# Changing the PSUM banks of three G_B tiles and of B's denominators in a gated mix of two linear-attention blocks

## The chip, the cores and the metric

The kernel runs on one core of one Trainium2 chip. The metric is the time of one execution on the device, in microseconds (us), given as the median of several runs. The core has a matrix engine (TensorE, PE in the profile; PEld is its row for weight loads), a vector engine (VectorE, DVE), a scalar engine (ScalarE, ACT), GpSimd (POOL) and a queue engine (SyncE, SP) that issues transfers. Matmuls write into PSUM, which this kernel holds as eight banks of 128 partitions x 512 fp32; ACT and DVE read results out of it ("evict" them) into SBUF.

## The reference

Both blocks see the same input x (2048 x 640, bf16), each with its own weights; 32 heads of 20 columns.

```python
def block(x, wqkv, wo):                      # A and B alike
    q, k, v = heads(x @ wqkv)                # H = 32, Dh = 20
    phi = lambda t: jnp.where(t > 0, t + 1, jnp.exp(t)) + 1e-6
    pq, pk = phi(q), phi(k)
    kv  = einsum("bhsd,bhse->bhde", pk, v)
    z   = einsum("bhsd->bhd", pk)
    num = einsum("bhqd,bhde->bhqe", pq, kv)
    den = einsum("bhqd,bhd->bhq", pq, z)[..., None] + 1e-6
    return merge(num / den) @ wo

g = sigmoid((x * gate_w).sum(-1, keepdims=True))
out = g * block(x, A_wqkv, A_wo) + (1 - g) * block(x, B_wqkv, B_wo)
```

## The kernel before, in words

The kernel never forms v. For each block X it computes PK = phi(k) in 16 row tiles (`k_tile`), PQ = phi(q) transposed in 20 tiles of 128 x 512 (`q_tile`), and G = x^T PK, a 640 x 640 matrix in five row tiles j (`g_piece`). From G it gets M = WV^T G, masked to the heads (`m_part`), then WP = M^T WO in five tiles (`wp_tile`), so that the result is one more matmul of PQ with WP (`fin_mm`). The denominators (`den`, line 637) are PQ times ZBD, the sums of PK spread out by head; DVE copies them out with eps added (line 652), takes four reciprocals (line 660), SP stores these and loads them back widened to all columns (`widen`, line 672), and DVE multiplies PQ by them (`scale`, lines 699 and 707). At the end `fin_a` (ACT, line 793) scales A's final tile by the gate, `fin_out` (DVE, line 805) adds B's, and SP stores the rows.

The eight PSUM banks are four pairs: `PP[0]` is banks 0 and 1 (the first pair), `PP[1]` banks 2 and 3, `PP[2]` banks 4 and 5, `PP[3]` banks 6 and 7 (the fourth pair). A G tile fills a pair: 512 columns in one bank and 128 in the other. It is built from four pieces q of eight matmuls (four row tiles, a 128x512 and a 128x128 matmul for each); after the fourth piece ACT evicts the whole tile to GT (line 577). A `wp_tile` also fills a pair, half a tile in each bank: ACT evicts the half in the first bank of the pair and DVE the one in the second (both line 759). Tiles 0 to 4 of WP A use the pairs 1, 2, 3, 1, 2 (line 891), those of WP B the pairs 0, 3, 1, 0, 3 (line 936). A's final tiles alternate between `PP[2]` and `PP[1]`, B's between `PP[0]` and `PP[3]` (line 768). Both halves of M_B use banks 7 and 6 (lines 932 and 933).

The order of work is that of the Python calls. A small scheduler (`_Sched`, line 72) records each call's reads and writes by key, PSUM keys being banks, and each engine runs its own operations in that order, waiting by semaphore for the last writer and all readers of what it touches; PE does not wait for PE (line 110). `_interleave` (line 192) deals out a list `mains` one entry at a time and slips in the stages of side chains at given positions. In `mains` the 20 q tiles of B come three at a time with one piece of G_B after each three, until five pieces are placed (line 884): the four of tile 0 and the first of tile 1. From `nB` on (line 885) the other 15 pieces of G_B follow (line 887). The chain at `nB + 1` (line 920) puts `wp_a_den_b` (line 889) behind the third piece of G_B's tile 1. So PE's order around the change is

- pieces 1 and 2 of G_B's tile 1; the five tiles of WP A; the denominators of B; piece 3 of tile 1, and its eviction
- the pieces of G_B's tiles 2, 3 and 4, while DVE scales A's queries
- A's final tiles 0 and 1, M_B, A's final tile 2, the five tiles of WP B, and then the final tiles of A and B in turn to the end

(pieces and tiles counted from 0 in the code; in words the tiles are the first to the fifth.) G_A, earlier in the kernel, uses the pairs 1, 0, 1, 0, 1 for its five tiles. All matmuls but the transposes are recorded by one helper, so the profile shows them under line 302, told apart by their operands: `ps<-PKB,XN` is G_B, `ps<-PQB,ZBD` the denominators of B, `ps<-WKA,MG` and `ps<-WKB,MG` WP A (its WO rows are kept in the old WK buffers), `ps<-GT,WVB` M_B, `ps<-WPA,PQA` the final tiles of A.

Of the kernel before, what the change touches and what calls it, by code (L numbers as in the profile page):

```python
# [205 lines left out]
def bass_gated_mix__linear_attn_block__linear_attn_block__prompt_kernel(  # L206
# [18 lines left out]
    with ExitStack() as es:  # L225
# [44 lines left out]
        def bank(i, lo, hi, p0=0, p1=128):  # L270
            o = 512 * (i % 2)
            return PP[i // 2][p0:p1, o + lo : o + hi]
# [23 lines left out]
        def mms(steps, reads=(), writes=(), name=""):  # L296


            def fn(pe):
                ins = None  # L300
                for o, l, r, st, sp, tp in steps:
                    ins = pe.matmul(o, l, r, start=st, stop=sp, tile_position=tp)  # L302
                return ins

            return sch.op("PE", fn, reads=reads, writes=writes, name=name)
# [5 lines left out]
        def act(fn, reads=(), writes=(), name=""):  # L311
            return sch.op("ACT", fn, reads=reads, writes=writes, name=name)

        def dve(fn, reads=(), writes=(), name=""):
            return sch.op("DVE", fn, reads=reads, writes=writes, name=name)
# [245 lines left out]
        def g_piece(X, j, q, pp):  # L561
            P = PP[pp]
            bks = [("PS", 2 * pp), ("PS", 2 * pp + 1)]
            steps = []
            for t in range(4 * q, 4 * q + 4):
                l = XN[:, t, 128 * j : 128 * j + 128]
                steps.append((P[:, 0:512], l, PK[X][:, t, 0:512], t == 0, t == NT - 1, None))
                steps.append((P[:, 512:D], l, PK[X][:, t, 512:D], t == 0, t == NT - 1, None))
            mms(
                steps,  # L570
                reads=[("XN", t) for t in range(4 * q, 4 * q + 4)] + [("PK", X, t) for t in range(4 * q, 4 * q + 4)],
                writes=bks,
                name="g%s%d%d" % (X, j, q),
            )
            if q == 3:
                act(
                    lambda e: e.activation(GT[:, j, :], P[:, 0:D], ACT.Copy),  # L577
                    reads=bks,
                    writes=[("GT", j)],
                )  # L580
# [56 lines left out]
        def den(X, bk):  # L637
            xi = BR.index(X)
            steps = []
            for k in range(NC):  # L640
                for b in range(NB):
                    o = bank(bk, 0, 512, 32 * b, 32 * b + 32)
                    r = PQ[X][:, k, 512 * b : 512 * b + 512]
                    steps.append((o, ZBD[:, NC * xi + k, :], r, k == 0, k == NC - 1, (0, 32 * b)))
            mms(
                steps,
                reads=[("ZBD", X)] + [("PQ", X, b, k) for k in range(NC) for b in range(NB)],
                writes=[("PS", bk)],
                name="den%s" % X,
            )  # L650
            dve(
                lambda e: e.tensor_scalar(DT32[:, :], bank(bk, 0, 512), EPS, None, op0=ALU.add),
                reads=[("PS", bk)],
                writes=[("DT",)],
            )

        def recip(i):
            def rcp(e):
                with nc.allow_low_precision(reason="r goes into a bf16 matmul"):
                    return e.reciprocal(RC[:, 128 * i : 128 * i + 128], DT32[:, 128 * i : 128 * i + 128])  # L660

            dve(rcp, reads=[("DT",)], writes=[("RC", i)])
# [76 lines left out]
        def wp_tile(X, k, pp):  # L739
            P = PP[pp]  # L740
            cells = []
            for g in range(4):
                w = 8 + g // 2 if k == 4 else 4 * (k // 2) + g
                fs = slice(32 * (g % 2), 32 * (g % 2) + 32) if k == 4 else slice(k % 2, 64, 2)
                cells.append((w, MG[:, w, fs]))
            for j, (lo, hi) in enumerate(((0, D // 2), (D // 2, D))):
                mms(
                    [
                        (P[32 * g : 32 * g + 32, 512 * j : 512 * j + hi - lo], l, wo_at(X, w)[0][:, lo:hi], True, True, (0, 32 * g))
                        for g, (w, l) in enumerate(cells)  # L750
                    ],
                    reads=[("WO", X, w) for w, _ in cells] + [("MG", w) for w, _ in cells],
                    writes=[("PS", 2 * pp + j)],
                    name="wp%s%d" % (X, k),
                )
            for j, (lo, hi) in enumerate(((0, D // 2), (D // 2, D))):
                o, p = WP[X][:, k, lo:hi], P[:, 512 * j : 512 * j + hi - lo]
                (dve if j else act)(
                    lambda e, o=o, p=p, j=j: e.tensor_copy(o, p) if j else e.activation(o, p, ACT.Copy),  # L759
                    reads=[("PS", 2 * pp + j)],  # L760
                    writes=[("WP", X, k, j)],
                )
# [105 lines left out]
        mains = []  # L868
# [9 lines left out]
        while qs:  # L878
# [3 lines left out]
            if len(qs) > 2:  # L882
                j, q = gs.pop(0)
                mains.append(lambda j=j, q=q: g_piece("B", j, q, 0))
        nB = len(mains)
        for j, q in gs:
            mains.append(lambda j=j, q=q: g_piece("B", j, q, 1 if j == 3 else 0))

        def wp_a_den_b():
            for k in range(NC):  # L890
                wp_tile("A", k, (1, 2, 3)[k % 3])
            den("B", 7)
            for i in range(4):
                recip(i)

        def den_a():
# [23 lines left out]
                nB + 1,  # L920
                [
                    (0, wp_a_den_b),
                    (0, lambda: widen("B")),
                ],
# [65 lines left out]
```

## Time and profile before

| what | us |
|---|---|
| median of 3 runs (lowest, highest) | 195.71 (195.59, 196.29) |
| the profiled execution, whole | 196.04 |
| its span, first to last instruction | 194.3 |
| PE busy | 188.1 (97% of the span) |
| DVE busy | 133.2 (69%) |
| ACT busy | 75.2 (39%) |
| POOL busy | 43.3 (22%) |

The granted PE clock is 0.999 of full speed over the span. Times in the profile are microseconds from the start of the span. A row of the timeline gives start, length, engine, line, operation, output <- inputs and how many were merged; in brackets stands how long the engine had been idle before it and what released it. A row of the waits gives who waited for whom, the total, the number of times and the longest. A row of the chain gives start, length and what the chain that ended last ran through. A matmul's row is longer than the distance to the next matmul's start, because successive matmuls overlap. A few per cent of matmul records are missing from a trace.

### The profile page before, as it was taken

The numbers are of one execution on the slowest core, as the hardware profiler recorded it, in microseconds if no ns is written. First come the engines' busy times: TensorE is split into PE (matmuls) and PEld (weight loads), VectorE is DVE, ScalarE is ACT, GpSimd is POOL, SyncE is SP. The second block draws the span as 40 slices with busy tenths as digits, with TensorE's granted clock in tenths as the row PEclk, the third lists the DMA queues.
The fourth block names the chain that finished last, engine by engine and source line by source line (L and its number), as shares of the span: only waits on it lengthen the run. The fifth ranks groups of instructions, "written<-read, shape, count | busy, mean of one in ns | idle before, by whom it ended". The sixth has DMA issues, their size and how long they took to land.

```text
span 194.3 us, 3541 instructions
## 1 busy us (share of the span) xinstructions
PE 188.1 (97%) x1402; PEld 103.8 (53%) x1428; DVE 133.2 (69%) x211; ACT 75.2 (39%) x130; POOL 43.3 (22%) x36
## 2 busy tenths in 40 slices
PE   8999999999999999999999999979999999999994
PEld 4655555555545554555465444435557555555552
DVE  0288899998997778786389877889631453452663
ACT  3366464656633342333322454340213632233301
POOL 1000223244237676656372000000000000000000
PEclk9999999999999999999999999999999999999999
DMA  5984479973400000000240017300134011111213
GB/s 187 312 139 99 94 189 370 366 254 91 114 9 0 3 0 0 0 0 24 63 128 3 0 37 202 115 2 20 48 117 141 34 67 45 59 67 67 71 67 101
DMA packets 20429, 18.02 MB, mean 93 GB/s; under 512 B 9211, under 2 KB 19644, under 8 KB 20412
## 3 DMA queue, kind: packets, MB, share of 16 engines
q1 hardware_dynamic: 19692, 17.05, 30.0%
q10 hardware_dynamic: 720, 0.74, 1.1%
q8 instruction: 11, 0.18, 0.4%
q14 instruction: 6, 0.05, 0.1%
HBM read 12.94 MB, written 2.88 MB: 81 GB/s over the span
## 4 chain that ended last, share of the span: by engine, by line
PE 93%; ACT 2%; DMA 1%; issue 1%; DVE 1%; DVEq 0%; ACTq 0%
PE ps L302 92%; DMA XN<-in_A_x_dram 1%; PE ps L425 1%; ACT WPB L759 1%; DVE WPA L759 1%; ACT PKA L793 0%; ACT GT L577 0%; DVE OSTG L805 0%; DVEq L960 0%; ACTq L158 0%
## 5 line engine op out<-in xcount | busy, mean ns | idle before, releaser
L536 ACT ACTIVATE EQ<-ps 128x512 bf16<-128x512 f32 x40 | 23.9, 597 | 39.5 <-PE ps L302 34.7
L541 DVE TENSOR_SCALAR EQ<-EQ 128x512 bf16<-128x512 bf16 x40 | 23.9, 597 | 15.0 <-ACT EQ L536 14.2
L495 ACT ACTIVATE EK<-ps 128x640 bf16<-128x640 f32 x32 | 22.4, 703 | 16.3 <-PE ps L302 15.7
L805 DVE SCALAR_TENSOR_TENSOR OSTG<-ps,SG,PKA 128x640 bf16<-128x640 f32 (+1 forms) x17 | 14.3, 844 | 20.6 <-PE ps L302 19.3
L302 PE MATMUL ps<-PKA,XN 128*128 128x128 bf16 (+1 forms) x157 | 24.4, 298 | 0.2
L302 PE MATMUL ps<-XT,WQA 128*128 128x512 bf16 x98 | 24.1, 379 | 0.1
L588 POOL TENSOR_TENSOR ZS<-ZS,PKA 128x640 f32<-128x640 f32 x13 | 18.6, 1427 | 24.9 <-DVE PKB L511 12.1
L793 ACT ACTIVATE PKA<-ps,SG 128x640 f32<-128x640 f32 x16 | 12.7, 795 | 28.9 <-PE ps L302 28.9
L302 PE MATMUL ps<-PKB,XN 128*128 128x128 bf16 (+1 forms) x157 | 22.7, 298 | 1.1 <-ACT GT L577 0.9
L302 PE MATMUL ps<-WPA,PQA 128*128 128x128 bf16 (+1 forms) x156 | 23.3, 297 | 0.3 <-ACT WPB L759 0.2
L302 PE MATMUL ps<-WPB,PQB 128*128 128x128 bf16 (+2 forms) x157 | 23.4, 298 | 0.2
L302 PE MATMUL ps<-WKA,XT 128*128 128x512 bf16 (+1 forms) x156 | 23.3, 302 | 0.2
L302 PE MATMUL ps<-WKB,XT 128*128 128x129 bf16 (+1 forms) x157 | 22.3, 298 | 0.2
L302 PE MATMUL ps<-XT,WQB 128*128 128x512 bf16 x96 | 22.2, 379 | 0.3 <-issue 0.2
L588 POOL TENSOR_TENSOR ZS<-ZS,PKB 128x640 f32<-128x640 f32 x13 | 18.4, 1418 | 11.6 <-DVE PQA L546 6.7
L302 PEld LDWEIGHTS ps<-PKA,XN 128*128 128x128 bf16 x160 | 13.0, 98 | 11.5
L302 PEld LDWEIGHTS ps<-PKB,XN 128*128 128x128 bf16 x160 | 12.4, 98 | 11.3 <-ACT GT L577 1.2
L302 PEld LDWEIGHTS ps<-WPA,PQA 128*128 128x128 bf16 x160 | 12.8, 98 | 9.7
L302 PEld LDWEIGHTS ps<-WPB,PQB 128*128 128x128 bf16 x160 | 12.9, 98 | 9.2
L302 PEld LDWEIGHTS ps<-WKB,XT 128*128 128x128 bf16 x160 | 12.4, 97 | 9.6
L302 PEld LDWEIGHTS ps<-WKA,XT 128*128 128x128 bf16 x160 | 12.5, 99 | 9.5 <-DVE XT L439 0.7
L506 DVE TENSOR_SCALAR EK<-EK 128x640 bf16<-128x640 bf16 x32 | 14.6, 457 | 2.1 <-ACT EK L495 1.9
(62 smaller groups left out, 156.1 us busy)
## 6 DMA issues: line engine op xcount, KB each, us to landing
out_dram<-OSTG SPq DMA_DIRECT2D x15, 160.0 KB, 1.8
XN<-in_A_x_dram SPq DMA_DIRECT2D x3, 640.0 KB, 8.7
PKA<-rsA SPq DMA_DIRECT2D x3, 480.0 KB
XT<-rsB SPq DMA_DIRECT2D x3, 360.0 KB
WKB<-in_B_wqkv_dram SPq DMA_DIRECT2D x1, 800.0 KB, 6.5
WQA<-in_A_wqkv_dram SPq DMA_DIRECT2D x1, 800.0 KB, 5.9
WVA<-in_A_wqkv_dram SPq DMA_DIRECT2D x1, 800.0 KB, 11.1
WQB<-in_B_wqkv_dram SPq DMA_DIRECT2D x1, 800.0 KB, 11.6
```

Source lines behind the costliest of these rows:

```text
L302: ins = pe.matmul(o, l, r, start=st, stop=sp, tile_position=tp)
L425: ins = pe.transpose(dst[:, 128 * i : 128 * i + 128], XN[:, t, 128 * c : 128 * c + 128], IDN[:, :],)
L495: lambda e: e.activation(EK[:, slot, :], P[:, 0:D], ACT.Exp),
L506: lambda e: e.tensor_scalar(EK[:, slot, :], EK[:, slot, :], 1.0, EPS, op0=ALU.min, op1=ALU.add),
L536: lambda e: e.activation(EQ[:, slot, :], bank(bk, 0, 512), ACT.Exp),
L541: lambda e: e.tensor_scalar(EQ[:, slot, :], EQ[:, slot, :], 1.0, EPS, op0=ALU.min, op1=ALU.add),
L588: lambda e: e.tensor_tensor(out=o, in0=a, in1=PK[X][:, t, :], op=ALU.add),
L759: lambda e, o=o, p=p, j=j: e.tensor_copy(o, p) if j else e.activation(o, p, ACT.Copy),
L793: lambda e: e.activation(TA[:, t % 5, :], PP[pp][:, 0:D], ACT.Copy, scale=SG[:, 0, t : t + 1]),
L805: lambda e, lo=lo, hi=hi, at=at: e.scalar_tensor_tensor(out=OSTG[:, slot, lo:hi], in0=PP[pp][:, at : at + hi - lo], scalar=SG[:, 1, t : t ...
```

## The change

```diff
         for j, q in gs:
-            mains.append(lambda j=j, q=q: g_piece("B", j, q, 1 if j == 3 else 0))
+            mains.append(lambda j=j, q=q: g_piece("B", j, q, (0, 0, 1, 0, 1)[j]))
 
         def wp_a_den_b():
             for k in range(NC):
                 wp_tile("A", k, (1, 2, 3)[k % 3])
-            den("B", 7)
+            den("B", 6)
             for i in range(4):
                 recip(i)
```

The last argument of `g_piece` is the pair. Before, G_B's five tiles use the pairs 0, 0, 0, 1, 0; after, 0, 0, 1, 0, 1. The first two tiles stay where they were. The denominators of B are accumulated in bank 6, the first bank of the fourth pair, in place of bank 7, its second; bank 6 held the half of WP A's third tile that ACT evicts, bank 7 the half that DVE evicts. No instruction is added, removed or moved in any engine's order; only the banks, and with them the waits, differ.

## The prediction

> **What bounds the kernel now.** I read the page first, for the busy shares and the chain that ended last; then the waits of all engines; then the chain in order of time between 124 and 153 us, where the edited calls run; and last the timeline of single engines around each gap.
>
> ```profile
> PE 188.1 (97%) x1402; PEld 103.8 (53%) x1428; DVE 133.2 (69%) x211; ACT 75.2 (39%) x130; POOL 43.3 (22%) x36
> ...
> PE 93%; ACT 2%; DMA 1%; issue 1%; DVE 1%; DVEq 0%; ACTq 0%
> ```
>
> TensorE (PE) carries 93% of the chain. A change that adds or removes no matmul can win only where PE stands still. The waits show how little of that there is: after the start-up these are all the waits of PE and its weight loads (PEld) of 0.3 us or more on another engine's tile.
>
> ```profile
> PEld ps L302 <- ACT GT L577: 1.2, 1, 1.2
> PE ps L302 <- ACT GT L577: 0.9, 1, 0.9
> PEld ps L302 <- DVE WPA L759: 0.3, 1, 0.3
> ```
>
> The first two are one event seen from PE's two rows. The chain places both events a few microseconds apart (start, length, what ran):
>
> ```profile
> 126.61 1.30 DVE WPA L759 x3
> 127.91 0.04 issue
> 127.95 1.26 PE ps L302 x20
> 129.22 0.16 issue
> 129.38 1.05 PE ps L302 x7
> 130.42 0.02 issue
> ...
> 130.51 0.71 ACT GT L577
> 131.22 0.05 issue
> 131.26 5.88 PE ps L302 x42
> ```
>
> The x20 piece is the denominators of B; the x7 piece is the last quarter of G_B's second tile (eight matmuls; its first record is missing); the x42 piece begins with G_B's third tile. Before the denominators PE waits for DVE's third eviction of WP A; before the third tile it waits until ACT has emptied the first pair of banks, because the second tile used that pair and the third uses it too.
>
> **Part 1: the third tile goes to the second pair.** Removed: PE's wait for the second tile's eviction. In the timeline PE runs the twelve pieces of tiles three to five from 131.26 to 144.31, where the next stage starts:
>
> ```profile
> 131.26 13.21 PE L302 MATMUL ps<-PKB,XN 128*128 128x512 bf16 x94 [0.85 <-ACT GT L577]
> 144.31 2.88 PE L302 MATMUL ps<-WPA,PQA 128*128 128x512 bf16 x20
> ```
>
> That is 13.05/12 = 1.088 us a piece from start to start, with two tile boundaries inside it whose waits were already met, so a met wait costs nothing. The last piece of tile two began at 129.16: its first recorded matmul, a 128x128 one, starts at 129.38, and a 128x512 one ahead of it takes 0.22 from start to start. At that pace the third tile could begin at 129.16 + 1.09 = 130.25 instead of 131.26: **1.01 us**. The 0.85 in the idle column is smaller, since the row of the last matmul (0.22 long, ended at 130.41) runs on for 0.16 after the next one could start. From that last start, 130.19, to 131.26 is 1.07, and no saving here can exceed it.
>
> The Trainium skill (Perfetto Trace Analysis, Identifying the Most-Contended Engine) says that a matmul's busy time is a poor measure because matmuls are pipelined. By a sum of the idle columns (0.85, and 0.08 between the last WP matmul's end at 127.87 and 127.95) the time would be 194.8; I take starts.
>
> What takes the wait's place: the second pair was last used by the fourth tile of WP A. ACT's fourth eviction starts at 127.44 and DVE's fourth at 127.81; at 0.45 and 0.48 us each both are done by 128.3, and the third tile's new turn is 130.25 (130.01 with part 3): 1.7 us of cover. Nothing else on PE's queue waits longer.
>
> **Part 2: the fourth tile goes to the first pair, the fifth to the second.** The fourth now waits for ACT's eviction of tile two (over at 131.21, earlier with part 3); its turn is 4 x 1.088 = 4.35 us after the third's, at 134.6. The fifth waits for tile three's eviction, which takes 0.70 plus some 0.3 from the last matmul's start, against 4.35 of matmuls between. Both cost 0. After tile five comes A's final tile 0 in the third pair, and then final tile 1, which uses the second pair: here is the one tight place. Before, it waited for tile four; now it waits for tile five, the tile just finished.
>
> ```profile
> 144.58 0.70 ACT L577 ACTIVATE GT<-ps 128x640 bf16<-128x640 f32 x1 [3.64 <-PE ps L302]
> 145.96 0.79 ACT L793 ACTIVATE PKA<-ps,SG 128x640 f32<-128x640 f32 x1 [0.68 <-PE ps L302]
> ```
>
> The eviction ends at 145.28; PE was released 0.05 us after an eviction's end at 131.21, so final tile 1 could start from 145.33. Its turn is halfway through the 20 matmuls from 144.31 to 147.03 (the next row's start), at 145.67. That leaves 0.34 us, and ACT stood idle for 3.64 us before, so the cost is 0; if the eviction came later than that, final tile 1, and behind it on PE M_B, final tile 2 and all of WP B would slip by the excess. M_B waited for the same eviction already. WP B's first tile, in the first pair, is released one tile earlier than before.
>
> **Part 3: the denominators of B go to bank 6.** The old wait is for the DVE half of the third WP A tile (bank 7), the new one for its ACT half (bank 6):
>
> ```profile
> 127.12 0.45 ACT L759 ACTIVATE WPA<-ps 128x320 bf16<-128x320 f32 x1
> 127.42 0.48 DVE L759 CAST WPA<-ps 128x320 bf16<-128x320 f32 x1
> ```
>
> ACT is done at 127.57, DVE at 127.90. With ACT's, the release would come near 127.61, and PE becomes the limit: the last four WP matmuls start 0.18 after those at 127.38, at 127.56, and a group of four takes 0.14 to 0.18. So the denominators can start at about 127.71 instead of 127.95: **0.24 us**. Bounds: 0 if another DVE result of that moment is still needed (none is: the scores and ZBD that they read are older than the evictions waited for before), 0.25 at best. The copy of the denominators, the four reciprocals and the store of them move with the matmuls. DVE's fifth WP eviction (start 128.21, 0.48) ends at 128.69, before that copy is due at 129.03. M_B's two bank users, in banks 7 and 6, come some 18 us later: 0.
>
> **What is late next.** Behind the fifth tile PE is driven by its own order up to WP B, where it waits for ACT's evictions (150.76 to 152.20 in the chain); those hang on PE's own matmuls and move along. From 152.32 to 190.32 the chain is PE alone. What does not move with PE is the transfer of B's reciprocals: DVE waited for it and finished the first scaling at 145.01 (144.59 + 0.42), while the M_B multiply queued behind it on DVE started at 148.76. PE comes 1.25 us sooner, the transfer 0.24: the slack falls from 3.75 to 2.7 and still covers it. The later scalings start at 158.62 and wait for no transfer.
>
> **Sum.** 1.01 + 0.24 = 1.25 us off the profiled execution's 196.04 (span 194.3 and 1.74 around it): 194.79. That execution lies 0.33 above the median of the three runs, so the median goes from 195.71 to **194.46**, 0.64% less. 0.5% is 0.98 us, about what a measurement here can tell from no change.
>
> **Rivals.**
> *Only the third tile's wait goes* (the denominators find another condition that ends near 127.9): 195.71 - 1.01 = 194.70, 0.52% less. Against it: PE's other inputs there are all older. 10%.
> *Part of the gain comes back at final tile 1.* If ACT's eviction of tile five comes late, its lag less 0.34 returns. The longest thing that could stand before it on ACT is one final-tile row, 0.79: return 0.45, time 194.9; with the whole 1.01 exposed it is 195.47. For it: the cover is only 0.34. Against it: ACT's order has nothing ahead of that eviction. 9%.
> *The wait stays* (the third tile finds the second pair unready): only part 3 is left, 195.47. Both evictions end 1.7 us early. 2%.
> *Slower: the PE clock drops while G_B alternates between two pairs.* At the start of the span matmuls ran slow: a 128x512 one starting at 4.12 took 0.63 and the next began at 4.57, 0.45 later, where it is 0.22 now. If tiles three to five ran at that pace, 13.05 us would become about 26 and the time about 207.5; a stretch like the first one (3.6 to 6.2) costs some 1.3 and ends at 195.7. It decides on the slower side of 0.5% once it loses 2.2 us, which is about 4.5 us at the slow pace. Against it: the granted clock is 1.00 in each stretch that I asked for from 62 to 104, where G_A alternates between the same two pairs, and the change makes PE's gaps shorter. 2%.
> The Trainium skill (TensorE: Matmul & The Clock Gate, A second HAM failure mode: psum-queue depth-cycling) reports such a drop in a kernel that cycles through banks with small gaps; by that rule this rival would win, and the trace of G_A disagrees with it here.
>
> **Chances and range.** The forecast has 77%, the rivals 10, 9, 2 and 2. The runs before spread from 195.59 to 196.29; the lowest less the best sum (1.07 + 0.25) is 194.27, and the second rival's mild form, 194.9, plus a scatter of 0.2 is 195.1. I take 194.2 to 195.1. Faster by over 0.5% needs 0.98 of the 1.25: the forecast's cases less those that scatter hides, and half of the first rival, 74%; within 0.5%, 23%; slower, 3%.
>
> **What would show it.** Right: PE's wait for ACT's GT gone; the third tile starts 1.09 us after the last piece of tile two; the denominators within 0.2 us of the last four WP A matmuls; final tile 1 directly behind final tile 0; PE's last matmul 1.25 us earlier. Wrong: a new PE wait for ACT GT near 144, a wait for an eviction of WP A at the third tile, matmul rows longer than 0.39 us in G_B, or DVE's M_B multiply held by the transfer.

## The result, and the profile after

The kernel after takes **194.64 us** (median of 6 runs, 194.43 to 194.88) against 195.73 of the kernel before (6 runs, 195.55 to 196.31), 1.09 us less; the ratio is 0.9937 with a 95% interval of 0.992 to 0.9954, that is 0.90 to 1.57 us less. The profiled execution took 194.64 with a span of 192.9.

On the page of the kernel after, PE's share of the chain has gone from 93% to 96%, and ACT's from 2% to under 1%:

```profile
PE 189.3 (98%) x1428; PEld 103.6 (54%) x1428; DVE 133.2 (69%) x211; ACT 75.2 (39%) x130; POOL 43.4 (22%) x36
...
PE 96%; DMA 1%; DVE 0%; ACT 0%; DVEq 0%; issue 0%; ACTq 0%
```

(PE's instruction count differs from before because that trace misses 26 matmul records; the order of every engine is the same.) In the waits of the kernel after, PE's waits for GT and for DVE's eviction of WP A are gone. These are the largest of PE that are left on another engine's tile:

```profile
PEld ps L302 <- DVE XT L439: 0.8, 2, 0.4
...
PEld ps L302 <- ACT WPA L759: 0.2, 1, 0.2
PEld ps L302 <- ACT WPB L759: 0.2, 1, 0.2
```

The timeline of PE shows the same place as one unbroken run (start, length, what):

```profile
127.05 0.71 PE L302 MATMUL ps<-WKB,MG 80*32 80x320 bf16 x11
127.58 1.25 PE L302 MATMUL ps<-PQB,ZBD 128*32 128x512 bf16 x20
128.77 14.30 PE L302 MATMUL ps<-PKB,XN 128*128 128x512 bf16 x104
142.91 2.88 PE L302 MATMUL ps<-WPA,PQA 128*128 128x512 bf16 x20
```

The x104 row is thirteen pieces of G_B, the last of tile two and the twelve of tiles three to five: (142.91 - 128.77)/13 = 1.088 us a piece, so the third tile follows at full pace. Before, the distance there was 131.26 - 129.16 = 2.10. The last four matmuls of WP A start at 127.45 (0.31 long, at the end of the first row, 127.76), and the denominators 0.14 later, where it was 0.39.

**A measure without the scatter.** The executions of one kernel differ by up to 1.2 us (the kernel before, 195.53 to 196.70 in 29 runs). In the traces the part of this that the edits do not touch has passed by the first matmul of WP A, which started at 126.10 before and 125.99 after, and between 125.57 and 126.40 in the eight executions below. I therefore also give a stretch S that holds both edits: from the first matmul of WP A to the first of WP B (`ps<-WKA,MG` to `ps<-WQA,MG` in the timeline). Its first and last row, before and after:

```profile
126.10 0.85 PE L302 MATMUL ps<-WKA,MG 80*32 80x320 bf16 x17
150.39 0.85 PE L302 MATMUL ps<-WQA,MG 80*32 80x320 bf16 x17
```

```profile
125.99 0.85 PE L302 MATMUL ps<-WKA,MG 80*32 80x320 bf16 x17
148.99 0.85 PE L302 MATMUL ps<-WQA,MG 80*32 80x320 bf16 x17
```

Before, S is 150.39 - 126.10 = 24.29; after, 148.99 - 125.99 = 23.00: 1.29 us less. From there to PE's last weight load it is 40.84 before and 40.83 after.

### The profile page after: what moved, and what is told of

Read it like the earlier page. It is cut to its first block, busy times and chain, and to the rows that moved or that the text cites. A ratio compares the mean times of both kernels' runs of the same rounds, so it can differ in the third digit from the quotient of the medians.

```text
span 192.9 us, 3567 instructions
## 1 busy us (share of the span) xinstructions
PE 189.3 (98%) x1428; PEld 103.6 (54%) x1428; DVE 133.2 (69%) x211; ACT 75.2 (39%) x130; POOL 43.4 (22%) x36
## 4 chain that ended last, share of the span: by engine, by line
PE 96%; DMA 1%; DVE 0%; ACT 0%; DVEq 0%; issue 0%; ACTq 0%
PE ps L302 95%; DMA XN<-in_A_x_dram 1%; PE ps L425 1%; ACT PKA L793 0%; DVE OSTG L805 0%; DVEq L960 0%; DVE XT L439 0%; ACTq L158 0%
## 5 line engine op out<-in xcount | busy, mean ns | idle before, releaser
L302 PE MATMUL ps<-PKA,XN 128*128 128x512 bf16 (+1 forms) x160 | 24.5, 299 | 0.0
L302 PE MATMUL ps<-WPA,PQA 128*128 128x512 bf16 (+1 forms) x160 | 24.2, 299 | 0.0
L302 PE MATMUL ps<-WPB,PQB 128*128 128x512 bf16 (+2 forms) x160 | 23.9, 299 | 0.0
L302 PE MATMUL ps<-XT,WQB 128*128 128x512 bf16 x100 | 23.0, 379 | 0.0
L302 PE MATMUL ps<-PKB,XN 128*128 128x512 bf16 (+1 forms) x160 | 22.9, 299 | 0.0
L302 PE MATMUL ps<-WKB,XT 128*128 128x512 bf16 (+1 forms) x160 | 22.5, 299 | 0.0
```

## The experiments

The theory is that of the prediction: each gap is PE's wait for the last reader of one pair or bank, and PE's order hands a saved gap on to the end. The first four kernels vary one edit each, with five rounds against the kernel before (median 195.98 of 29 runs beside them; ratios are to these).

**One edit without the other: the tiles.**

```diff
-            den("B", 6)
+            den("B", 7)
```

> Only the pairs of G_B change (0, 0, 1, 0, 1); the denominators stay in bank 7. Theory (each gap is the wait for the last reader of one pair, and PE's order hands all of a saved gap on to the end): the gap before the third tile goes, the one before the denominators stays; from the last piece of tile two to the third tile 1.09 us between starts in place of 2.11, from the last four matmuls of WP A to the denominators 0.39 to 0.40 as before; 1.01 us less than before, 0.24 more than with both edits, about 194.7 to 194.9. Rival (the two waits hang together, one edit without the other gives little): within 0.3 us of the kernel before.

195.08 us, ratio 0.995 (0.9934 to 0.9966). S is 23.26, 1.03 less than before. In its chain the wait for DVE's third eviction is back and no wait for GT shows:

```profile
126.66 1.30 DVE WPA L759 x3
127.95 0.04 issue
128.00 1.26 PE ps L302 x20
129.26 0.16 issue
129.42 6.74 PE ps L302 x49
```

The theory holds; the rival falls. The time itself is above the 194.7 to 194.9 expected, as the kernel before took 195.98 beside it and not 195.73.

**The other edit alone: the denominators.**

```diff
-            den("B", 7)
+            den("B", 6)
```

(against the kernel before)

> Only the denominators move to bank 6; G_B keeps the pairs 0, 0, 0, 1, 0. Theory: the denominators start 0.13 to 0.15 us after the last four matmuls of WP A instead of 0.40, everything behind them comes 0.25 us sooner, and the gap before the third tile stays at 2.11 us from start to start; about 195.5. Rival (the wait before the third tile takes up what is gained ahead of it): the third tile's gap grows by 0.25 and the time is that of before.

195.77 us, ratio 0.9991 (0.9981 to 1.0001): by time alone not to be told from the kernel before. S tells it: 24.03, 0.26 less. Its chain runs through WP A and the denominators without a stop, and the gap before the third tile is as long as it was, so the rival falls:

```profile
130.23 0.02 issue
130.25 0.02 ACTq L158
130.26 0.04 issue
130.31 0.71 ACT GT L577
131.02 0.05 issue
131.07 5.88 PE ps L302 x42
```

The two edits add up: 1.03 + 0.26 = 1.29, which is what both together take off S.

**The fifth tile back in the fourth's pair.**

```diff
-            mains.append(lambda j=j, q=q: g_piece("B", j, q, (0, 0, 1, 0, 1)[j]))
+            mains.append(lambda j=j, q=q: g_piece("B", j, q, (0, 0, 1, 0, 0)[j]))
```

> As after, but the fifth tile of G_B stays in the first pair, where the fourth is: pairs 0, 0, 1, 0, 0. Theory (the price is paid wherever two successive tiles share a pair): the gap moves from the third tile to the fifth, about 2.1 us from the start of the last piece of tile four to the start of tile five, PE waits for ACT's GT once; 1.01 us more than after, 195.65. Rival (the cost belongs to the third tile's place, next to the denominators and the reciprocals): no gap before the fifth tile and a time within 0.3 us of after.

195.43 us, ratio 0.9976 (0.9963 to 0.9988); S is 24.03, 1.03 more than after. The gap has moved to the fifth tile, at its old size:

```profile
136.80 2.34 PE L302 MATMUL ps<-PKB,XN 128*128 128x512 bf16 x16
140.00 1.21 PE L302 MATMUL ps<-PKB,XN 128*128 128x512 bf16 x7 [0.86 <-ACT GT L577]
```

So it belongs to two successive tiles in one pair, wherever they stand, and not to the place beside the denominators.

**A final tile of A directly behind the fifth tile in its pair.**

```diff
-            return {"A": (2, 1), "B": (0, 3)}[X][t % 2]
+            return {"A": (1, 2), "B": (0, 3)}[X][t % 2]
...
-            wp_tile("B", k, (0, 3, 1)[k % 3])
+            wp_tile("B", k, (0, 3, 2)[k % 3])
```

> As after, with A's even final tiles in the second pair and the odd ones in the third (and the third tile of WP B in the third pair, so that its pair is free as before). The first final tile of A now directly follows the fifth tile of G_B in the same pair. Theory: PE waits there for ACT's eviction of the fifth tile, 1.02 us more between starts, and the whole of it shows in the end: 195.65. Rival of the prediction (cover is not what matters there, ACT's eviction does not hold PE at this place): within 0.3 us of after.

195.60 us, ratio 0.9984 (0.9972 to 0.9996); S is 24.10, 1.10 more than after. The gap has moved again, to the final tile:

```profile
143.00 0.71 ACT GT L577
143.71 0.14 issue
143.84 1.24 PE ps L302 x5
```

The wait costs here what it costs elsewhere, plus 0.07: from the eviction's end to PE's start there are 0.14 us in place of 0.05. Most of the difference is in the trace: PE's sequencer has a semaphore instruction of its own there (line 158, 0.05 us, at 143.74), and none before the third tile in the kernel before. The order of the pairs after G_B is therefore part of the gain: with it changed, the whole gain of the third tile is gone.

S is read from one trace of each kernel. In all six kernels of this section that have five rounds, what S and the stretch behind it show lies inside the interval of the ratio; for the fifth tile, for instance, 0.26 less than before, where the interval says 0.24 to 0.73.

**What the gap consists of.** In two kernels ACT reads a G_B tile twice; the copy goes to a buffer that nothing reads. Each was run once (196.31 and 194.60 us), so only S is compared; the second lies below the kernel after only because it reached WP A 0.41 sooner. The first is the kernel before with the second tile read twice.

```diff
             if q == 3:
+                if X == "B" and j == 1:
+                    act(
+                        lambda e: e.activation(EK[:, 0, :], P[:, 0:D], ACT.Copy),
+                        reads=bks,
+                        writes=[("EK", 0)],
+                    )
```

> The kernel before (pairs 0, 0, 0, 1, 0), with the second tile of G_B read out by ACT twice: a copy of the same size into a buffer that is free then, and behind it the eviction. Theory (the gap before the third tile is the drain of the last matmul, ACT's eviction and the release, one behind the other): the gap grows by one more eviction, 0.65 to 0.70, from 2.11 to 2.76 to 2.81 us between the starts of the last piece of tile two and tile three, and the stretch from the first WP A matmul to the first WP B matmul from 24.29 to 24.94 to 24.99. Rival (PE waits there for something else that ends by chance near ACT's eviction): the stretch stays at 24.29.

S is 24.97, 0.68 more. In the chain the two reads stand one behind the other, with PE released 0.05 after the second:

```profile
130.01 0.71 ACT EK L578
130.72 0.02 issue
130.74 0.71 ACT GT L583
131.46 0.05 issue
131.50 0.66 PE ps L302 x3
```

So the gap holds the whole eviction and grows with it. It grows by 0.68 and not by the 0.73 between the starts of the two reads, because the first read began 0.05 sooner behind the last piece than in the kernel before (130.01 - 128.71 = 1.30 against 130.51 - 129.16 = 1.35).

The second is the kernel after with the fifth tile read twice (the same edit with `j == 4`), to measure the cover of the tight place.

> The kernel after, with the fifth tile of G_B read out by ACT twice. Theory (the first final tile of A covers the eviction with 0.34 us to spare): the release of the second final tile comes 0.65 to 0.70 later, so PE now waits there for 0.31 to 0.36, and the stretch from the first WP A matmul to the first WP B matmul grows from 23.00 to 23.31 to 23.36. Rival (more cover than worked out): it stays at 23.00; rival (no cover at all): it grows by the whole 0.65 to 0.70.

S is 23.35, 0.35 more, as the theory has it and between the two rivals. The timeline of PE shows the new wait at the second final tile, 1.69 us behind the first instead of 1.36:

```profile
142.50 1.52 PE L302 MATMUL ps<-WPA,PQA 128*128 128x512 bf16 x10
144.19 1.53 PE L302 MATMUL ps<-WPA,PQA 128*128 128x512 bf16 x10 [0.17 <-ACT GT L583]
```

The eviction itself stands so in the kernel after (first line) and here (second line):

```profile
143.17 0.70 ACT L577 ACTIVATE GT<-ps 128x640 bf16<-128x640 f32 x1 [3.64 <-PE ps L302]
143.43 0.70 ACT L583 ACTIVATE GT<-ps 128x640 bf16<-128x640 f32 x1
```

In the kernel after it ends 0.96 us behind the first final tile's start (143.87 - 142.91), here 1.64 behind it: 0.68 later. PE lost 0.34 of this, so the cover was about 0.34 us.

**Two attempts at a better version.** Between 125.99 and 127.58 the ten groups of WP A take 1.60 us where an undisturbed group takes 0.135. The first attempt puts a piece of G_B between them.

```diff
-        def wp_a_den_b():
-            for k in range(NC):
+        def wp_a():
+            for k in range(3):
+                wp_tile("A", k, (1, 2, 3)[k % 3])
+
+        def wp_a_den_b():
+            for k in range(3, NC):
                 wp_tile("A", k, (1, 2, 3)[k % 3])
...
-                    (0, wp_a_den_b),
+                    (0, wp_a),
+                    (1, wp_a_den_b),
```

> The kernel after, with the last piece of G_B's tile two moved between the third and the fourth tile of WP A, so that the evictions of WP A have 1.09 us of matmuls to catch up in. Theory (the last three groups of WP A and the denominators still wait a little for evictions, 1.60 us for ten groups that need 1.36): the stretch from the first WP A matmul to the first WP B matmul goes from 23.00 to about 22.77; 194.4. Rival (the third tile of G_B now waits for the fourth WP A tile's evictions, which stand behind the eviction of tile two on ACT): a new wait in front of the third tile, and 23.0 or more.

194.52 us, ratio 0.9931 (0.9917 to 0.9945); S is 23.00, the same as after. Neither theory nor rival: the waits inside WP A are gone and no new wait costs PE time, yet nothing is gained. (The waits put 0.4 us of idle time before the third tile's first weight load down to DVE's eviction of WP A. But that had ended 0.3 us earlier, and in the kernel before the first weight load behind the denominators has the same 0.42, as `issue`.) The timeline says why:

```profile
126.26 0.31 PE L302 MATMUL ps<-WKB,MG 80*32 80x320 bf16 x3
126.50 1.26 PE L302 MATMUL ps<-PKB,XN 128*128 128x512 bf16 x8
127.69 0.31 PE L302 MATMUL ps<-WKA,MG 80*32 80x320 bf16 x1
```

From the last WP group to the piece of G_B it is 0.24 from start to start where 0.135 is usual, and the piece takes 1.19 to the next WP group in place of 1.088. Each change between the narrow matmuls (32 columns of weights) and the full ones (128) costs PE about 0.10 us, and the spread order has two more of them. Beside them its ten groups take 0.83 + 0.56 = 1.39 us in place of 1.60: 0.21 is gained and 0.21 lost. The Trainium skill (TensorEngine Tiling (Array Packing), Key Properties) states that changing the tiling mode drains the TensorE; the 0.10 at each change here fits it, though no trace shows the draining itself.

The second attempt spreads WP B too, with A's final tiles one step further ahead.

```diff
-        for k in range(NC):
-            wp_tile("B", k, (0, 3, 1)[k % 3])
-        fin_a(2)
-        fin_mm("A", 3)
-        fin_a(3)
+        for k in range(2):
+            wp_tile("B", k, (0, 3)[k % 2])
+        fin_a(2)
+        fin_mm("A", 3)
+        for k in range(2, NC):
+            wp_tile("B", k, (0, 3)[k % 2])
+        fin_a(3)
+        fin_mm("A", 4)
+        fin_a(4)
...
-            if 0 < t < NT - 4:
-                fin_mm("A", t + 3)
-                fin_a(t + 3)
+            if 0 < t < NT - 5:
+                fin_mm("A", t + 4)
+                fin_a(t + 4)
```

> As the one with WP A spread, and WP B's tiles spread as well: two, then A's final tile 3, then three, then A's final tile 4, with A's final tiles one step further ahead from there. Theory: ten groups of WP B take 1.36 us beside the final tile instead of 1.70, and nothing waits for their evictions; from the first WP A matmul to the last one of the kernel 0.23 + 0.34 = 0.57 us less than after, 63.27 instead of 63.84; time 194.05. Rival (the evictions of WP B are the limit of that stretch in any order, DVE needing 0.40 us for each half): 0.3 less at most, all of it from WP A.

195.14 us, ratio 0.9961 (0.9947 to 0.9975): 0.40 us worse behind S (41.24 from the first WP B matmul to PE's last weight load, against 40.83), with S at 23.00 as in the first attempt. Two more changes of matmul shape cost 0.2, and the last WP B tile stands in the pair of the one two before it, so that PE waits for ACT's eviction; from 151.63 to 152.16 it is 0.53 where a group takes 0.135. That is 0.6 lost, and the waits of WP B in the old order, which are gone, gave only 0.2 back:

```profile
151.63 0.30 PE L302 MATMUL ps<-PKA,MG 80*32 80x320 bf16 x3
152.16 0.46 PE L302 MATMUL ps<-PKA,MG 80*32 80x320 bf16 x8 [0.23 <-ACT WPB L759]
```

The expectation missed both. No version that is measurably better than the kernel after came out of this.

## Why the prediction was right

**The third tile.** Forecast 1.01; the distance from the last piece of tile two to the third tile went from 2.10 to 1.09, and the edit alone took 1.03 off S. Counting from start to start, and not by the idle column's 0.85, was right. The Trainium skill (Perfetto Trace Analysis, Identifying the Most-Contended Engine) says that the busy share of matmuls is no good measure of how close a kernel is to its limit, as they are pipelined; the trace agrees in that idle time between them misleads too, with 1.03 lost where 0.85 shows.

**The fourth and fifth tile, and final tile 1.** Forecast 0, with 0.34 us of cover at final tile 1. Measured by the doubled read, the cover is about 0.34. The place was as tight as told, and one more read of ACT there shows in the end.

**The denominators.** Forecast 0.24 with 0.25 at best; their start behind WP A went from 0.39 to 0.14, and S lost 0.26 with that edit alone. The DVE half of WP A's third tile was all that held them.

**What is late next.** Nothing on PE's path. DVE's first scaling of B still waits for its transfer and ends at 144.79, and the M_B multiply behind it starts at 147.35: a slack of 2.56 where 2.7 was told, since PE came 1.29 sooner behind WP A's start and the transfer only 0.12 where 0.24 was told.

```profile
144.36 0.43 DVE L707 TENSOR_TENSOR PQB<-PQB,XT 128x512 bf16<-128x512 bf16 x1 [1.12 <-DMA XT<-rsB]
147.35 0.89 DVE L729 TENSOR_TENSOR MG<-ps,CB 80x512 bf16<-80x512 f32 x2 [2.57 <-PE ps L302]
```

**The sum.** 1.25 was forecast, 1.29 is what S lost, and the profiled executions lie 1.40 apart because the one after also reached WP A 0.11 sooner. The medians moved by 1.09, so that 194.64 lies 0.18 above the 194.46 told; the interval of the ratio holds both 1.25 and 1.29. The traces do not hold the runs that make the medians; that the difference is scatter ahead of WP A, as in the profiled executions, is likely and not shown.

**The rivals.** Each edit alone gave its own part, and both together the sum, so the gain is not the third tile's alone. A return at final tile 1 does not happen as the kernel stands, and does with 0.7 us more on ACT. The third tile found its pair ready. PE's clock did not drop while G_B alternates: a piece takes 1.088 there as before, and a 128x512 matmul 0.38. The granted clock of 1.00 from 129 to 143 says less than the prediction took it for, since in the kernel before it also reads 1.00 from 3 to 6, where such a matmul took 0.63. The Trainium skill (TensorE: Matmul & The Clock Gate, A second HAM failure mode: psum-queue depth-cycling) tells of a drop where PE idles briefly and often between groups that cycle through banks; this trace, in which the alternation leaves no idle time on PE, shows none.

## What to carry to other kernels

Where the matrix engine carries the chain, look for two successive accumulations into the same PSUM bank: each costs the whole way of the last matmul, the eviction and the release (here 1.0 us for 128x640), and a single other block of matmuls between them hides it if it is longer (here a final tile of 1.36). Measure such a gap from matmul start to matmul start, and follow each new neighbour of the pairs to the end of the stage, since the wait goes wherever two neighbours meet. When the runs scatter by more than the effect, time a stretch inside the trace that holds the edit.

## What the runs showed of the hardware that was not expected

Each change between narrow matmuls (80x32 or 128x32 weights) and full ones cost about 0.10 us of PE time, also where nothing was waited for: the denominators' last group to the next piece of G_B in the kernel after, and each of the added changes in the spread kernels. From 80x32 to 128x32 it cost nothing: the denominators start 0.14 behind WP A's last group, as one group does behind another.

The scatter between executions, as far as the traces hold it, arises in the first 10 us, with the speed of the first matmuls. The matmuls on GWR, at 8.76 to 9.59 us, start 116.81 before the first of WP A in each of the ten traces. A 128x512 matmul near 4.1 us took 0.63 in the kernel after and 0.45 in the one with the final tiles swapped, which was the faster one up to WP A by 0.18 us (125.81 against 125.99):

```profile
4.14 0.63 PE L302 MATMUL ps<-const-bfloat16-1.0 128*128 128x512 bf16 x1
```

```profile
4.13 0.45 PE L302 MATMUL ps<-const-bfloat16-1.0 128*128 128x512 bf16 x1
```

The Trainium skill (TensorE: Matmul & The Clock Gate, What's actually happening) explains such a start by a clock that is released at the end of a free-running window, and so at another moment in each execution; these traces agree in that the slow matmuls end at different times.
